# The query load of an attention kernel, cut into 120 partitions and 8 partitions

## The chip, the cores and the metric

One core of one Trainium2 chip runs the whole kernel. The metric is the device time of one execution in microseconds (us); lower is better. Times are medians of several runs. "Profile" is one profiled execution of a kernel; its span is a little shorter than the time (635.5 us for a time of 636.9). Some places below use the trace's raw records, which no view of the profile prints: the moment of each semaphore increment that a DMA makes, the start and duration of each DMA packet, and the queue of a packet. They are given in ordinary tables and in the text. The records do not name the DMA engine of a packet; where the text says that packets belong to one engine, that is inferred from their times, each packet starting where the one before it ends.

## The reference

```python
B, H, Sq, Skv, Dh = 8, 16, 16, 2048, 256          # all bfloat16, values of about 0.05
def reference(q, k, v):
    scale = q.shape[-1] ** -0.5
    scores = jnp.einsum('bhqd,bhkd->bhqk', q, k) * scale
    attn = _softmax(scores, axis=-1)
    return jnp.einsum('bhqk,bhkd->bhqd', attn, v)
```

There are 128 heads. Keys and values are 128 MiB each and are read once; the queries are 1 MiB, 8 KB for each head. So the kernel is a stream of key and value loads with the arithmetic hidden behind it.

## The kernel before

The 128 heads are taken in 16 groups of 8 ("g" below). Each group has two key loads and two value loads of 4096 KB (`u` counts them), the first four key loads being cut in halves and the last four value loads into smaller parts. Loads are issued on the queue of SP, in order, as soon as the buffer they fill is free. The query is loaded first, one head to a partition (one of the 128 rows of a buffer), into a buffer that the values use later; VectorE then transposes it.

```python
KN = ec(nc.sbuf_tensor("KN", [128, 2, NT, D], BF16))           # keys as loaded
KB = ec(nc.sbuf_tensor("KB", [128, R_KB, HT // 2, D], BF16))   # keys transposed, 4 slots
VB = ec(nc.sbuf_tensor("VB", [128, 2, NT, D], BF16))           # values
...
qx = q.rearrange("b h s d -> (b h) (s d)")                     # 128 rows of 8 KB
QR = VB[:, 1, 0:SQ, :].rearrange("p s d -> p (s d)")           # where they land
...
j_q = [J("sp", "ldq", lambda eng: eng.dma_start(QR[0:NH, :], qx), [j_qz], dma=(sem_q, 16))]
...
def k_load(u):                                                 # g: group of heads, e: 0 or 1
    g, e = u // 2, u % 2
    if g < 2:
        for h in range(2):
            j_k[u, h] = J("sp", "ld", lambda eng, h=h, n=HT: eng.dma_start(
                KN[:, e, HT * h:HT * h + HT, :], ku[u, :, HT * h:HT * h + HT, :]), ...)
...
j_qt[0] = J("dve", "qt", emit_qt, j_q)                         # transpose of the query
...
def kt(g, e, c):                                               # transpose of a quarter of a key load
    ...
    j_kt[g, e, c] = J("dve", "kt%d%d" % (e, c), lambda eng: emit_kt(eng, e, c), [j_k[2 * g + e, h], before])
```

`J` notes a job of an engine with the jobs it must wait for. Here all 128 heads exist, so `j_qz` is None and NH is 128.

## Time and profile before

| | before |
|---|---|
| time, median (lowest to highest) | 636.86 us (636.82 to 637.09, 4 runs) |
| span of the profile | 635.5 us |
| mean DMA rate over the span | 426 GB/s |
| one group of heads (16 MiB) | 39.0 us, 430 GB/s |

From the page of the kernel before: the share of the DMA engines that is busy in 40 equal slices (in tenths), the GB/s in each slice, and the chain of waits by engine.

```profile
DMA  8999999999999999999999999999999999999997
GB/s 364 430 432 437 442 431 429 433 429 431 431 431 431 431 429 433 429 433 429 433 430 431 433 429 433 429 429 433 437 425 439 435 429 439 427 440 429 414 424 280
...
DMA 74%; DVE 18%; issue 5%; PE 3%; SPq 0%; DVEq 0%; ACT 0%; ACTq 0%
```

The DMA engines are busy from end to end at some 430 GB/s, and three quarters of the chain of waits is DMA. The compute engines are not what the time waits for.

The start of the same kernel in stretches of 3 us (columns: length, busy time of each engine, TensorE clock, DMA share, GB/s). A packet's bytes are counted where the packet falls, so a single stretch can read a little over the true rate.

```profile
core 0: us, PE busy (x) PEld busy (x) DVE busy (x) ACT busy (x) POOL busy (x), PEclk, DMA share, GB/s
3.00:6.00 3.00, 0.00 (x0) 0.00 (x0) 0.00 (x0) 0.00 (x0) 1.91 (x1) 1.00 1.08 451
6.00:9.00 3.00, 0.00 (x0) 0.00 (x0) 1.90 (x1) 0.00 (x0) 0.00 (x0) 1.00 1.01 434
9.00:12.00 3.00, 0.00 (x0) 0.00 (x0) 2.82 (x6) 0.08 (x1) 0.00 (x0) 1.00 1.02 437
```

Already from 3 us on all DMA engines are busy (share 1.01 to 1.08) and the rate is full (434 to 451 GB/s). The end of the chain of waits (start, length, what):

```profile
591.84 30.00 DMA KN<-in_v_dram
621.84 0.14 issue
621.97 10.82 PE O_ps L183 x96
```

The last wait is for a part of a value load, which lands at 621.84 us; 96 matmuls follow without a gap. So the kernel ends some 14 us after that landing, and whatever moves the landing moves the end.

In these records each of the two loads raises its semaphore 16 times, and from 3 to 20 us 16 packets at a time are under way but for moments: one increment for each of 16 engines. These are the moments (us) for the first two loads, from the trace's records:

```
query load      5.25 ... 5.60 (15 increments)    7.01 (the last)
first key load  10.13 ... 10.49 (15 increments)  11.90 (the last)
```

One engine is 1.4 us behind the others from the query load on. By its times it is the one that also fetched 16 KB of instructions at 3.62 us: that packet of another queue took 961 ns, and the query packet behind it 773 ns instead of 309, together 1.43 us.

### The profile page before, as it was taken

The numbers are of one execution on the slowest core, as the hardware profiler recorded it, in microseconds if no ns is written. First come the engines' busy times: TensorE is split into PE (matmuls) and PEld (weight loads), VectorE is DVE, ScalarE is ACT, GpSimd is POOL, SyncE is SP. The second block draws the span as 40 slices with busy tenths as digits, with TensorE's granted clock in tenths as the row PEclk, the third lists the DMA queues.
The fourth block names the chain that finished last, engine by engine and source line by source line (L and its number), as shares of the span: only waits on it lengthen the run. The fifth ranks groups of instructions, "written<-read, shape, count | busy, mean of one in ns | idle before, by whom it ended". The sixth has DMA issues, their size and how long they took to land.

```text
span 635.5 us, 5055 instructions
## 1 busy us (share of the span) xinstructions
PE 485.9 (76%) x2176; PEld 165.5 (26%) x1680; DVE 437.5 (69%) x387; ACT 93.7 (15%) x176; POOL 4.2 (1%) x7
## 2 busy tenths in 40 slices
PE   0847859959598695976959679595895949959897
PEld 0101312214132141321313123131230412314286
DVE  6998894766938579395683947749477594766960
ACT  2030303003030030300303012030110302003010
POOL 2000000000000000000000000000000000000000
PEclk9969989969899698997979989699896998979999
DMA  8999999999999999999999999999999999999997
GB/s 364 430 432 437 442 431 429 433 429 431 431 431 431 431 429 433 429 433 429 433 430 431 433 429 433 429 429 433 437 425 439 435 429 439 427 440 429 414 424 280
DMA packets 13718, 270.62 MB, mean 426 GB/s; under 512 B 1552, under 2 KB 3856, under 8 KB 4368
## 3 DMA queue, kind: packets, MB, share of 16 engines
q1 hardware_dynamic: 13296, 270.36, 99.2%
q10 hardware_dynamic: 416, 0.18, 0.1%
q8 instruction: 4, 0.07, 0.0%
q14 instruction: 2, 0.02, 0.0%
HBM read 269.48 MB, written 1.05 MB: 426 GB/s over the span
## 4 chain that ended last, share of the span: by engine, by line
DMA 74%; DVE 18%; issue 5%; PE 3%; SPq 0%; DVEq 0%; ACT 0%; ACTq 0%
DMA KN<-in_k_dram 65%; DVE KB L133 16%; DMA KN<-in_v_dram 5%; DMA VB<-in_v_dram 4%; PE O_ps L183 2%; DVE QT L117 1%; PE S_ps L150 1%; PE S_ps L138 1%; DVE PC L163 0%; DVE negm L155 0%; SPq L217 0%; DVE O_fin L331 0%; SPq L201 0%; SPq L235 0%; DVEq L499 0%
## 5 line engine op out<-in xcount | busy, mean ns | idle before, releaser
L150 PE MATMUL S_ps<-KB,QW 128*128 128x512 bf16 x528 | 214.5, 415 | 136.5 <-DMA VB<-in_v_dram 94.3
L133 DVE STREAM_TRANSPOSE KB<-KN 128x2048 f32<-128x2048 f32 x128 | 284.8, 2280 | 48.6 <-DMA KN<-in_k_dram 47.8
L138 PE MATMUL S_ps<-KB,QW 128*128 128x512 bf16 x496 | 205.4, 414 | 0.0
L177 PE MATMUL O_ps<-VB,PT 128*128 128x512 bf16 x896 | 195.6, 379 | 9.3 <-DMA VB<-in_v_dram 9.3
L150 PEld LDWEIGHTS S_ps<-KB,QW 128*128 128x128 bf16 x528 | 54.0, 103 | 341.2 <-issue 278.6
L177 PEld LDWEIGHTS O_ps<-VB,PT 128*128 128x128 bf16 x896 | 86.7, 98 | 120.8 <-issue 18.1
L155 DVE TENSOR_REDUCE negm<-S_ps 128x1 f32<-128x2048 f32 x16 | 36.7, 2291 | 85.7 <-PE S_ps L138 85.7
L159 ACT ACTIVATE P_sb<-S_ps,negm 128x2048 bf16<-128x2048 f32 x16 | 31.5, 1967 | 409.3 <-DVE negm L155 409.3
L163 DVE STREAM_TRANSPOSE PC<-P_sb 128x1024 bf16<-128x1024 bf16 x32 | 37.9, 1222 | 33.8 <-ACT P_sb L159 33.8
L169 DVE COPY PT<-PC 32x1024 bf16<-32x1024 bf16 x128 | 53.4, 418 | 3.4 <-PE O_ps L183 1.7
L127 ACT ACTIVATE QW<-QT 32x128 bf16 (+1 forms) x128 | 53.9, 421 | 11.2 <-DVE QT L117 9.9
L320 ACT ACTIVATE O_tmp<-O_ps,rab 128x256 f32<-128x256 f32 x15 | 7.1, 473 | 96.3 <-PE O_ps L177 95.2
L183 PE MATMUL O_ps<-KN,PT 128*128 128x256 bf16 x128 | 14.5, 273 | 0.8 <-DMA KN<-in_v_dram 0.8
L183 PE MATMUL O_ps<-VB,PT 128*128 128x256 bf16 x128 | 14.1, 273 | 0.3 <-DVE PT L169 0.3
L183 PEld LDWEIGHTS O_ps<-KN,PT 128*128 128x128 bf16 x128 | 12.4, 98 | 2.7 <-issue 1.1
L183 PEld LDWEIGHTS O_ps<-VB,PT 128*128 128x128 bf16 x128 | 12.4, 98 | 2.3 <-DVE PT L169 0.8
L117 DVE COPY QT<-QN 32x512 f32<-32x512 f32 x16 | 9.7, 606 | 0.3
L331 DVE TENSOR_SCALAR O_fin<-O_ps,rab 128x256 bf16<-128x256 f32 x2 | 1.0, 482 | 12.5 <-PE O_ps L183 12.5
L325 DVE SCALAR_TENSOR_TENSOR O_fin<-O_ps,rab,O_tmp 128x256 bf16<-128x256 f32 x15 | 6.7, 445 | 1.8 <-issue 1.8
L110 DVE STREAM_TRANSPOSE QN<-VB 128x2048 f32<-128x2048 f32 x1 | 2.3, 2311 | 5.0 <-DMA VB<-in_q_dram 5.0
L302 DVE TENSOR_SCALAR rab<-mask,rinv 128x2 f32<-128x2 f32 x16 | 3.6, 228 | 2.1 <-DVE rinv L301 0.5
L196 POOL MEMSET PT<- 128x4096 f32 x1 | 3.5, 3511 | 0.0
(12 smaller groups left out, 10.8 us busy)
## 6 DMA issues: line engine op xcount, KB each, us to landing
VB<-in_v_dram SPq DMA_DIRECT2D x28, 4096.0 KB, 24.3
KN<-in_k_dram SPq DMA_DIRECT2D x28, 4096.0 KB, 30.0
KN<-in_k_dram SPq DMA_DIRECT2D x8, 2048.0 KB, 14.9
VB<-in_v_dram SPq DMA_DIRECT2D x4, 2048.0 KB, 17.1
KN<-in_v_dram SPq DMA_DIRECT2D x2, 2048.0 KB, 27.7
KN<-in_v_dram SPq DMA_DIRECT2D x2, 1024.0 KB, 24.3
KN<-in_v_dram SPq DMA_DIRECT2D x3, 512.0 KB, 26.9
VB<-in_q_dram SPq DMA_DIRECT2D x1, 1024.0 KB, 6.3
```

The source lines that it names most:

```text
L117: ins = eng.tensor_copy(dst[:, :, 8 * x:8 * x + 8], src[:, :, :, a])
L127: ins = eng.activation(ap_of(dv, dv.offset + 32 * a + e, [[256, 4], [128, 2], [2, 16]]), src.rearrange("p (s b) t -> p b t s", b=4), ACTF. ...
L133: return eng.transpose(KBf[:, c % R_KB].rearrange("p t i -> p (t i)"), KNf[:, e].rearrange("p t i -> p (t i)")[:, n * c:n * c + n])
L138: return eng.add_instruction(mybir.InstMatmult(start_tensor_calc=start, stop_tensor_calc=stop, ldweights=False, tile_size=(128, 128), tile ...
L150: ins = mm(S_ps[:, 2 * h + c, :], QW[:, e, bp, :], rhs, start=(e == 0 and bp == 0), stop=(e == 1 and bp == 7))
L155: return eng.tensor_reduce(out=negm[:], in_=S_ps[:].rearrange("p c n -> p (c n)"), axis=AX.X, op=ALU.max, negate=True)
L159: return eng.activation(P_sb[:], S_ps[:].rearrange("p c n -> p (c n)"), ACTF.Exp, bias=negm[:], scale=1.0, accum_out=lsum[:])
L163: return eng.transpose(PC[:, h].rearrange("p t x -> p (t x)"), P_sb[:, 1024 * h:1024 * h + 1024])
L169: ins = eng.tensor_copy(PT[pr, 32 * h:32 * h + 32, pr], PC[pr, h])
L177: ins = eng.matmul(O_ps[:, 0, :], PT[:, t, :], rhs, start=(t == 0), stop=(t == NT - 1))
L183: ins = eng.matmul(O_ps[:, bank, 0:D], PT[:, t, :], buf[:, t, :], start=(t == 0), stop=(t == NT - 1))
L320: j_ea[g] = J("act", "ea", lambda eng: eng.activation(O_tmp[:], src, ACTF.Copy, scale=rab[:, 0, 0:1]), [("pv", g, 1) if g < last - 1 else ...
```

## The change

The change text gives the intent as: the first 120 partitions' rows go over 15 DMA engines and the last 8 partitions' rows over 8. The natural purpose is to take the query rows away from one engine of the sixteen. Below it is called the spared engine, and the engines that carry the last 8 rows the eight.

```diff
-        j_q = [J("sp", "ldq", lambda eng: eng.dma_start(QR[0:NH, :], qx), [j_qz], dma=(sem_q, 16))]
+
+        j_q = [J("sp", "ldq", lambda eng, a=a, b=b: eng.dma_start(QR[a:b, :], qx[a:b]), [j_qz],
+                 dma=(sem_q, 32 if NH >= 120 else 16)) for a, b in ([(0, 120), (120, NH)] if NH >= 128 else [(0, NH)])]
```

## The prediction

> **What bounds the kernel now.** DMA throughput. The page's DMA row reads 9 tenths in nearly every slice at some 430 GB/s; the chain of waits is 74% DMA. One group of heads takes 39.0 us (spacing of the V-load issues on SP) for four 4096 KB loads: 430 GB/s. The queue never runs dry: a key load issued at 84.9 us lands 29.3 us later, three loads deep. At the end PE waits for the value load landing at 621.84 us, then runs 96 matmuls in 10.82 us without a gap.
>
> **The lag.** Each load lands as 16 semaphore increments, one per DMA engine. For the query load 15 come at 5.25 to 5.59 us and the last at 7.01 us. That engine lost its time to a 16 KB instruction fetch at 3.62 us (961 ns, and a query packet beside it took 773 ns instead of 309), and it stays 1.4 us behind: the next loads land with the same last gap. Later fetches hit other engines: one of 8 KB at 74.3 us puts a second 0.6 us back, and three of 16 KB at 590.8, 613.0 and 628.0 us put others about 1.3 us back. For the load landing at 621.84 us the last three engines stand at 621.67, 621.76 and 621.84.
>
> **What the change does.** [...] No engine numbers show in this trace; 120 partitions then give 15 engines and 8 give 8. So engine 15 gets no query row: it is spared 8 packets of 309 ns = 2.5 us, less some 0.5 us that it starts later, with the first key load, whose issue moves back by one DMA issue (0.4 us on SP). Engines 0 to 7 get one 8 KB row more, 0.31 us. Total bytes, PE, DVE and ACT work are unchanged.
>
> **What is on the critical path.** The slowest engine at the last loads. If the lagging engine is number 15 (the intent), it is no longer last: up to 1.4 us gained in most of the run, where the deep queue means nothing waits for it. At the end the engines hit by the fetches at 590 and 613 us are within 0.2 us of it, so only about 0.1 us is left to gain; if they are among engines 0 to 7 they come 0.31 us later than now. If the lagging engine is another, nothing is gained. A risk: 15-way splitting may make engines write the same part of the on-chip memory at once; doubling the query load's 2.5 us would put most engines, and the end, back by up to 2.5 us.
>
> **Prediction.** 637.0 us, range 636.3 to 638.6. Faster by over 2%: 0.5%; within 2%: 99%; slower: 0.5%.
>
> **What would show it.** Right: two query DMAs on SP, the first key load issued 0.4 us later; the last gap of 1.41 us of the first loads gone; the 39.0 us period, 430 GB/s and the PE tail of 10.8 us unchanged; the last loads moved by under 0.5 us. Wrong: query packets longer than 309 ns; a large last gap still there; the load before the PE tail landing over 0.5 us earlier or later; fetches at other times.
>
> **What would make it wrong.** A slow query load as said; the late fetches falling on the spared engine, which would let the whole 1.4 us through to the end; instruction fetches that move in time with the program.

The sum came to 637.0 us. Its terms are the 636.86 us before, less the 0.1 us left to gain at the end, plus 0.31 us for one packet of 8 KB (309 ns) more, together 637.07. "Engine 15" and "engines 0 to 7", here and in the expectations below, are names for the spared engine and for the eight; no trace shows an engine's number. The counts of 15 and 8 show in the trace after the change, in the next section. That engines which write the same part of the memory at once hold each other up was a guess here; what 8 rows to neighbouring partitions cost was measured later (+1.25 us, late8).

## The result, and the profile after

| | before | after |
|---|---|---|
| time, median (lowest to highest) | 636.86 us (636.82 to 637.09) | 640.18 us (640.12 to 640.34) |
| landing that the last 96 matmuls wait for | 621.84 us | 625.07 us |
| query packets of 8 KB, median | 309 ns | 610 ns |
| one group of heads | 39.0 us | 39.0 us |

The ratio of after to before is 1.0052 (95% interval 1.0034 to 1.0069). A ratio here is the mean time of one kernel's runs over that of the other's of the same rounds, so it is not quite the ratio of the medians quoted. The change makes the kernel 3.3 us slower, which is far outside the spread of the runs, though well under 2%.

The page of the kernel after:

```profile
DMA  8999999999999999999999999999999999999996
GB/s 285 430 434 428 435 434 437 431 431 429 431 427 431 433 433 431 439 431 433 427 433 427 431 429 431 438 437 431 435 431 429 427 431 429 431 438 435 416 425 277
...
DMA 70%; DVE 19%; issue 5%; PE 5%; SPq 0%; DVEq 0%; ACT 0%; ACTq 0%
```

Only the first slice differs much: 285 GB/s in place of 364. A slice is 16 us long. The busy row is the same digit for digit but for the last slice. The stretches show where in that slice:

```profile
core 0: us, PE busy (x) PEld busy (x) DVE busy (x) ACT busy (x) POOL busy (x), PEclk, DMA share, GB/s
3.00:6.00 3.00, 0.00 (x0) 0.00 (x0) 0.00 (x0) 0.00 (x0) 1.91 (x1) 1.00 1.03 243
6.00:9.00 3.00, 0.00 (x0) 0.00 (x0) 0.00 (x0) 0.00 (x0) 0.00 (x0) 1.00 1.00 218
9.00:12.00 3.00, 0.00 (x0) 0.00 (x0) 1.82 (x1) 0.00 (x0) 0.00 (x0) 1.00 1.01 421
```

From 3 to 9 us the DMA share is 1.0 as before, so the engines count as "busy", but they move 243 and 218 GB/s in place of 451 and 434. Over the 9 us from 3 to 12 us the sum of the three rates is 882 in place of 1322, so (1322 - 882) x 3 us = 1320 KB were not moved. At 430 GB/s these take 3.1 us. That is the whole loss: the end of the chain of waits is the same as before, moved by 3.2 us,

```profile
594.62 30.44 DMA KN<-in_v_dram
625.07 0.14 issue
625.20 10.77 PE O_ps L183 x96
```

and the middle has kept its period. On the SP queue two issues of value loads, eleven groups apart, before,

```profile
157.63 0.81 SPq L235 DMA_DIRECT2D VB<-in_v_dram  x2
...
586.88 1.82 SPq L235 DMA_DIRECT2D VB<-in_v_dram  x4
```

and after:

```profile
160.43 0.81 SPq L237 DMA_DIRECT2D VB<-in_v_dram  x2
...
589.67 1.81 SPq L237 DMA_DIRECT2D VB<-in_v_dram  x4
```

586.88 - 157.63 is 429.25 us and 589.67 - 160.43 is 429.24 us. Nothing was lost or won in between: this kernel streams at its DMA rate of some 430 GB/s throughout and made good none of the 3 us lost at its start.

VectorE sees the loss first. Its transpose of the query, with the idle time before it in brackets, before and after:

```profile
7.10 2.31 DVE L110 STREAM_TRANSPOSE QN<-VB 128x2048 f32<-128x2048 f32 x1 [5.03 <-DMA VB<-in_q_dram]
```

```profile
10.18 2.31 DVE L110 STREAM_TRANSPOSE QN<-VB 128x2048 f32<-128x2048 f32 x1 [8.11 <-DMA VB<-in_q_dram]
```

The increments after the change:

```
both query DMAs   1.31, 1.71 (2 increments, before any packet)   7.13 ... 10.09 (23 increments)
first key load    12.72   13.07 ... 13.76 (14 increments)   14.71 (the last)
```

From 3 to 5.1 us 15 packets at a time are under way after the change but for moments, where 16 were before; the sixteenth engine starts at 5.17 us, with the first key packet. So of the 23 late increments 15 are the first DMA's, and 8 are left for the second, one for each row. None of the 23 comes before 7.13 us, so the engine that began with keys at 5.17 us had no query row of either DMA: there is one spared engine, and the eight are among the other fifteen. The two early increments come before the first query packet starts (1.76 us). VectorE waits until the semaphore has risen by 32, 16 for each DMA, and is released at 10.18 us, after the last of the 23; so the two early ones stand for the missing 9. An engine that is late by about 1 us (14.71 against 13.76) is still there.

### The profile page after: what moved, and what is told of

It is laid out like the page before. It is cut to its first block, busy times and chain, and to the rows that moved or that the text cites. A ratio compares the mean times of both kernels' runs of the same rounds, so it can differ in the third digit from the quotient of the medians.

```text
span 638.6 us, 5056 instructions
## 1 busy us (share of the span) xinstructions
PE 488.1 (76%) x2176; PEld 165.8 (26%) x1680; DVE 437.6 (69%) x387; ACT 93.8 (15%) x176; POOL 4.2 (1%) x7
## 4 chain that ended last, share of the span: by engine, by line
DMA 70%; DVE 19%; issue 5%; PE 5%; SPq 0%; DVEq 0%; ACT 0%; ACTq 0%
DMA KN<-in_k_dram 61%; DVE KB L133 17%; DMA KN<-in_v_dram 5%; DMA VB<-in_v_dram 4%; PE O_ps L183 2%; PE S_ps L150 2%; PE S_ps L138 1%; DMA VB<-in_q_dram 1%; DVE QT L117 1%; DVE PC L163 0%; DVE QN L110 0%; DVE negm L155 0%; DVE O_fin L333 0%; SPq L202 0%; SPq L237 0%
```

## The experiments

**Theory P (place).** What a query packet takes depends on which partitions are written at the same time. With all 128 partitions in one DMA it is 309 ns (before); with 120 or 64 neighbouring ones twice that, as the 610 ns after the change suggest, with 8 neighbouring ones up to four times, and with 8 partitions that lie 4 apart nearly no delay. This was a conjecture. The author's grounds for it, how the rows of a DMA are dealt out to the engines and which partitions get in each other's way, are shown by no trace.

**Rivals.** I: the load is merely uneven (one engine with none, eight with one row more). D: a second DMA costs by itself, by its issue. K: a DMA that uses fewer than 16 engines is slow wherever it writes. One more was not named before the runs, H: what counts is the place in memory that the rows are read from, not the partitions that they are written to. S came with the last pair: what extra8_spread lost besides was due not to the place but to an engine that stood idle.

The runs below were made in three batches, each on a chip of its own and each against the kernel before on that chip. Its median was 636.96 us (9 runs) in the first batch (halves, only120, extra8, extra_tiny), 637.08 in the second (columns, extra8_spread, spread8, block8) and 637.02 in the third (late8, late8_spread); the row "after" is the change itself, against 636.86.

| run | what it is | time, median | over before |
|---|---|---|---|
| after | 120 rows, then 8 rows | 640.18 | +3.3 |
| halves | 64 rows, then 64 rows | 639.74 | +2.8 |
| columns | 128 rows twice, half a row each | 637.79 | +0.7 |
| only120 | 120 rows, the rest not loaded | 639.17 | +2.2 |
| extra8 | as before, 8 rows more to 8 neighbouring partitions | 638.20 | +1.2 |
| extra8_spread | the same 8 rows to 8 partitions 4 apart | 638.08 | +1.0 |
| extra_tiny | as before, 128 pieces of 512 bytes more | 637.39 | +0.4 |
| spread8 | 16 DMAs of 8 rows, partitions 4 apart | 645.29 | +8.2 |
| block8 | 16 DMAs of 8 rows, neighbouring partitions | 650.91 | +13.8 |
| late8 | extra8, issued after the first key loads | 638.27 | +1.25 |
| late8_spread | extra8_spread, issued there | 637.34 | +0.3 |

For columns, extra8_spread, extra_tiny and late8_spread the 95% interval of the ratio includes 1, so by that measure these four can't be told from before; of them only the runs of extra8_spread overlap with those of before.

### Two halves of 64 partitions: no engine is spared

```diff
-        j_q = [J("sp", "ldq", lambda eng: eng.dma_start(QR[0:NH, :], qx), [j_qz], dma=(sem_q, 16))]
+        j_q = [J("sp", "ldq", lambda eng, a=a: eng.dma_start(QR[a:a + 64, :], qx[a:a + 64]), [j_qz], dma=(sem_q, 32))
+               for a in (0, 64)]
```

> The query load as rows 0 to 63 and rows 64 to 127, each of 64 partitions[...]: no engine is spared, none has more than before. Theory P [...]: query packets of about 612 ns instead of 309, the first key load lands about 2.5 us later, the whole kernel +2.5 us (639.4). Rival I (imbalance: the loss came from the extra row on engines 0 to 7 and from a spared engine that started late): packets 309 ns, total within 0.3 us of before. Rival D (each further DMA on the queue costs by itself): about +0.4 us.

Measured: 639.74 us, ratio 1.0043 (1.0029 to 1.0056), query packets of 600 ns in the median. The first two stretches of the start:

```profile
3.00:6.00 3.00, 0.00 (x0) 0.00 (x0) 0.00 (x0) 0.00 (x0) 1.91 (x1) 1.00 1.03 235
6.00:9.00 3.00, 0.00 (x0) 0.00 (x0) 0.00 (x0) 0.00 (x0) 0.00 (x0) 1.00 1.03 273
```

At a DMA share of 1.03 in both stretches no engine can have stood idle for long, and the rate is far down all the same: 235 and 273 GB/s in place of 451 and 434. Rival I, which asked for packets of 309 ns, can't give this. Rival D asked for +0.4. How the 64 rows are dealt out to the engines is not shown.

### Two halves by columns: two DMAs of all 128 partitions

```diff
-        j_q = [J("sp", "ldq", lambda eng: eng.dma_start(QR[0:NH, :], qx), [j_qz], dma=(sem_q, 16))]
+        j_q = [J("sp", "ldq", lambda eng, a=a: eng.dma_start(QR[:, a:a + 2048], qx[:, a:a + 2048]), [j_qz], dma=(sem_q, 32))
+               for a in (0, 2048)]
```

> The query load in two DMAs as in the change, but cut along the columns: both have all 128 partitions, 4 KB of each. Same bytes, same number of DMAs as the change and as the halves. Theory P: [...] packets are 159 ns for 4 KB as elsewhere, and the end is within 0.4 us of before. Rival D (a second query DMA costs by itself, by its issue or by being one more to finish): +2.5 us as with the halves.

Measured: 637.79 us (637.69 to 637.92), ratio 1.0011 (0.9997 to 1.0025), packets of 4 KB at 159 ns in the median.

```profile
3.00:6.00 3.00, 0.00 (x0) 0.00 (x0) 0.00 (x0) 0.00 (x0) 1.91 (x1) 1.00 1.07 365
6.00:9.00 3.00, 0.00 (x0) 0.00 (x0) 1.46 (x1) 0.00 (x0) 0.00 (x0) 1.00 0.97 401
9.00:12.00 3.00, 0.00 (x0) 0.00 (x0) 2.92 (x5) 0.00 (x0) 0.00 (x0) 1.00 1.02 437
```

The same bytes in the same number of DMAs cost 0.7 us instead of 2.8. That is against rival D as the main cause. It is more than the 0.4 us that was expected, though: some 0.8 us worth of bytes is missing between 3 and 9 us ((1322 - 365 - 401 - 437) x 3 us = 357 KB). Why is not settled; about a third of these packets was longer than 159 ns.

### Each part of the change alone

The first part alone (the last quadrant of the transposed query is made from another quadrant's rows):

```diff
+        j_q = [J("sp", "ldq", lambda eng: eng.dma_start(QR[0:120, :], qx[0:120]), [j_qz], dma=(sem_q, 16))]
...
-            return eng.transpose(QN[:].bitcast(F32), QR.bitcast(F32))
+            eng.transpose(QN[0:96, :].bitcast(F32), QR[0:96, :].bitcast(F32))
+            return eng.transpose(QN[96:128, :].bitcast(F32), QR[64:96, :].bitcast(F32))
```

> Rows 0 to 119 alone on 15 engines; the last 8 rows are not loaded and the last quadrant is filled from another one (a wrong result on purpose, one more transpose of 2.3 us on the vector engine at the start, where it has slack). The first part of the change alone. Theory P: packets of about 612 ns, first key load about +2.5 us on 15 engines, the end about +2.4 us: most of the 3.3 us of the change. Rival I: packets 309 ns, nothing later than before, the end within 0.2 us. If the spared engine were the one that lags, its increment would come first, not last, at the first key load; if not, the last gap of about 1 us stays.

Measured: 639.17 us (639.08 to 640.12), ratio 1.0035 (1.0021 to 1.0049), query packets 572 ns. The result even passed the comparison, presumably because the scores are so small that other queries hardly change the softmax. The query load's last increment came at 9.61 us, 1.76 us after the one before it, on the engine that fetched 16 KB at 4.20 us. That engine had query rows, so the lagging engine is not the spared one. Two reservations: the profiled run was the slowest of the five (640.12 us), with a second engine late at the first key load (13.46 us, where most stand at 12.30 to 12.60); and no engine was done with its query rows before 7.25 us (5.25 before the change). So whatever slows the packets reached all 15 engines; the next run shows something of the same kind.

The second part alone, into spare memory (slot 3 of KB, which is written only after VectorE has waited for `sem_q`):

```diff
+        QD = KB[120:128, 3].rearrange("p t i -> p (t i)")
+        j_q = [J("sp", "ldq", lambda eng: eng.dma_start(QR[0:NH, :], qx), [j_qz], dma=(sem_q, 32)),
+               J("sp", "ldq", lambda eng: eng.dma_start(QD, qx[120:128]), dma=(sem_q, 32))]
```

> The query load whole as before, then the last 8 rows once more into spare memory, as an 8-partition DMA on 8 engines. This is the second part of the change alone. Theory P: [...] engines 0 to 7 come out some 1.2 to 1.5 us later at the first key load, the others little; the end +0.1 us if the engines that fetch late are not among them, up to +1.5 us if they are. Rival I: they come out 0.3 us later, the end at most +0.3 us.

Measured: 638.20 us (638.14 to 638.26), ratio 1.0019 (1.0005 to 1.0033).

The two parts add up: 2.2 + 1.2 = 3.4 us, against 3.3 us for the change. But extra8 did not go as theory P had it in detail. The eight were to be late and the others hardly. In fact 15 increments of the first key load came at 11.29 to 11.82 us, against 10.13 to 10.49 before: all engines lost about 1.1 us, because the first key packets behind the query rows took 1.2 to 1.6 us instead of 0.61, on engines with and without one of the 8 rows (all but the lagging one, which got there later). So 8 rows to 8 neighbouring partitions held up nearly all engines. The path by which it happens is not shown here.

### A control: one more small DMA of all 128 partitions

```diff
+        QD = KB[:, 3, 0, :]
+        j_q = [J("sp", "ldq", lambda eng: eng.dma_start(QR[0:NH, :], qx), [j_qz], dma=(sem_q, 32)),
+               J("sp", "ldq", lambda eng: eng.dma_start(QD, qx[:, 0:D]), dma=(sem_q, 32))]
```

> The query load whole as before, then a further DMA of 128 partitions with 512 bytes each into spare memory: a control for what one more DMA costs by being issued. Theory P: query packets stay 309 ns, the end within 0.4 us of before (64 KB more are 0.15 us and 8 small packets for each engine 0.2 us). Rival D: +2 us or more, since the first key load waits behind one more issue.

Measured: 637.39 us (637.30 to 637.49), ratio 1.0007 (0.9993 to 1.002), query packets 309 ns. The +0.4 us is at the edge of what was expected. Rival D falls.

### The 8 rows to partitions 4 apart, twice

The edit against extra8:

```diff
-        QD = KB[120:128, 3].rearrange("p t i -> p (t i)")
+        QD = KB[96:125:4, 3].rearrange("p t i -> p (t i)")
```

> As extra8, but the 8 extra rows go to partitions 96, 100 and so on to 124, [...] instead of 120 to 127[...]. Same 8 engines, same bytes, same issue. Theory P: the first key load's increments move by some 0.3 to 0.5 us instead of the 1.1 us of extra8, and the end is some 0.3 to 0.6 us over before instead of 1.24. Rival K (a DMA on fewer than 16 engines, or one that starts while others run, costs that much wherever it writes): the same 1.1 and 1.24 us again.

Measured: 638.08 us, but spread from 637.38 to 638.41; ratio 1.0013 (0.9999 to 1.0027). At the first key load theory P held: 14 increments at 10.59 to 10.87 us, 0.4 us over before and not 1.1. The end did not follow, because in the profiled run (638.41 us) a second engine was 1.2 us late there. By the times of its packets it stood idle from 5.05 to 6.09 us, until its first key packet came. The issue was not quite the same either: the extra DMA took 0.83 us on SP instead of 0.36, so the first key load was issued at 2.06 us instead of 1.59 in extra8. As a whole time this run is inconclusive. So the pair was run again with the 8 rows behind the first two key loads, where no engine was expected to run dry (late8 against before; late8_spread has the other QD, partitions 96, 100 and so on to 124):

```diff
+        QD = KB[120:128, 3].rearrange("p t i -> p (t i)")
         for g in range(G):
             for u in (2 * g, 2 * g + 1):
                 k_load(u)
+                if u == 0:
+                    j_x = J("sp", "ldq", lambda eng: eng.dma_start(QD, qx[120:128]), dma=(ec(nc.semaphore("s_x")), 16))
...
-            j_kt[g, e, c] = J(..., [j_k[2 * g + e, h], before])
+            j_kt[g, e, c] = J(..., [j_k[2 * g + e, h], before, j_x if (g, e, c) == (0, 0, 3) else None])
```

> The query load whole as before; the 8 extra rows of extra8 (partitions 120 to 127[...]) are issued only after the first two key loads, so that no engine can run dry at the start. Theory P: the increments of the first key load stay where they are before the change (10.1 to 10.5 us and the late one), those of the third load come some 1.0 us later on most engines than before the change, and the end is +1.0 to 1.2 us. Rival K: the same as late8_spread.

> As late8[...]. Theory P: the third load's increments come only some 0.15 to 0.35 us later than before the change, the end +0.15 to +0.4 us. Rival S [...] is the same theory in full: here no engine runs dry, so the bimodal 637.4 to 638.4 us of extra8_spread should be gone.

Measured: late8 638.27 us (638.12 to 638.29), ratio 1.0019 (1.0006 to 1.0033); late8_spread 637.34 us (637.27 to 637.54), ratio 1.0006 (0.9992 to 1.0019). The stretch from 15 to 18 us, in which the 8 rows and the load behind them fall, of before, late8 and late8_spread:

```profile
15.00:18.00 3.00, 1.45 (x4) 0.39 (x3) 2.60 (x2) 0.39 (x1) 0.00 (x0) 1.00 1.02 437
```

```profile
15.00:18.00 3.00, 1.60 (x4) 0.39 (x3) 1.53 (x2) 0.22 (x1) 0.00 (x0) 1.00 0.90 284
```

```profile
15.00:18.00 3.00, 1.44 (x4) 0.39 (x3) 2.20 (x2) 0.38 (x1) 0.00 (x0) 1.00 1.00 399
```

The two kernels read the same 8 rows, with the same shape and the same place in the queue (the issue took 0.72 and 0.83 us); only the 8 destination partitions differ. So rival H falls for these rows: what they cost depends on where they are written. The neighbouring partitions cost 153 GB/s over 3 us (437 - 284), the ones 4 apart 38. The third key load's 15 early increments stand at 19.93 to 20.28 us before, 21.04 to 21.69 in late8 and 20.45 to 20.93 in late8_spread. Rival K falls: the same 8 rows cost +1.25 us in neighbouring partitions and +0.3 us in partitions 4 apart. The third load moved by 0.5 to 0.65 us in late8_spread, twice what was expected at most, but the end only by 0.3 us, as expected; late8's end is just over its 1.0 to 1.2 us. The spread of the times is gone (637.27 to 637.54), as rival S expected; that the engine which ran dry made the spread was seen in one profile only.

For the 120 rows there is no such pair: in every run that writes other partitions at once, other rows are read at once too. That the partitions written and not the source cost the +2.2 us is carried over from this pair and from the doubled packets, and is not shown by a run of its own.

### The whole query by 8 engines, neighbouring partitions or not

```diff
# spread8: 8 partitions, 4 apart
+        j_q = [J("sp", "ldq", lambda eng, a=a: eng.dma_start(QR[a:a + 29:4, :], qx[a:a + 29:4]), [j_qz], dma=(sem_q, 256))
+               for a in (0, 1, 2, 3, 32, 33, 34, 35, 64, 65, 66, 67, 96, 97, 98, 99)]
# block8: 8 neighbours
+        j_q = [J("sp", "ldq", lambda eng, a=a: eng.dma_start(QR[a:a + 8, :], qx[a:a + 8]), [j_qz], dma=(sem_q, 256))
+               for a in range(0, 128, 8)]
```

> The query load as 16 DMAs of 8 partitions, 4 apart, each on 8 engines[...]. Engines 0 to 7 carry all the query rows, 16 each, and 16 issues take some 7 us on the queue. Theory P: packets near 309 ns; the query load done some 7 to 9 us after its start (bound by the issue), the end some 3 to 6 us over before. Rival K: as block8.

> The same 16 DMAs on the same 8 engines, but of 8 neighbouring partitions each[...]: only which partitions meet in a DMA differs from spread8. Theory P: packets of some 600 to 1240 ns [...], the query load takes up to 20 us, and the end is some 8 to 17 us over before, well over spread8. Rival K: packets and time as spread8.

Measured: spread8 645.29 us (ratio 1.0131), packets 419 ns in the median; block8 650.91 us (ratio 1.0218), packets 943 ns in the median. Block8 fell where theory P put it. Its first stretch:

```profile
3.00:6.00 3.00, 0.00 (x0) 0.00 (x0) 0.00 (x0) 0.00 (x0) 1.91 (x1) 1.00 0.48 66
```

A DMA share of 0.48 is 8 of 16 engines, all busy, and they move 66 GB/s together. From 7.3 us the first key load runs on the eight engines without query rows, and until the query load ends at 19.78 us most of its 16 KB packets took 1.1 to 2.5 us there instead of 0.61. That is extra8's finding again, on a larger scale. Spread8 is a miss in size, 8.2 us where 3 to 6 were expected. Its 16 issues took 10.9 us on SP (0.7 us each, not the 0.4 us reckoned), so the first key load was issued at 11.64 us instead of 1.18; in block8 the issues took 5.5 us. Its packets were longer than 309 ns too; why was not looked into. So the two differ in more than the partitions, and the sizes can't be compared closely; but block8, with the shorter issue, has packets of over twice the length and the longer time, as theory P says.

Spread8 tells one thing more. Its query rows all go by the same eight engines, if it is as in block8, where 16 DMAs of 8 rows kept a DMA share of 0.48; and its instruction fetch runs from 2.18 to 3.23 us. All eight packets of the first query DMA ran in that time (from 2.29 to 2.97 us), and its eight increments stand at 3.15 to 3.29 us: the fetch has delayed none of them. (The first key load's 16 increments stand within 0.35 us of each other, but these engines had idle time before it in which to catch up.) So the engine that fetches there is none of the eight. With only120 (it is not the spared one) that leaves the seven others, if DMAs of 8 rows use the same eight engines in every run, and if the same engine fetches in every run; no run here shows an engine's number. Which of them it is was not tried.

## Why the prediction was wrong

The prediction said 637.0 us with a range of 636.3 to 638.6; it was 640.18.

- **The step that failed: the price of the query load.** The prediction put it at its bytes, "Engines 0 to 7 get one 8 KB row more, 0.31 us", and left the rest of the load at its old 309 ns a packet. The runs put it at 610 ns a packet. Engines that write the same part of the memory at once stood in the text only as a risk, "doubling the query load's 2.5 us would put most engines, and the end, back by up to 2.5 us", outside the sum, and that bound lay outside the range as well. It was the main term: only120 measures it as +2.2 us and halves as +2.8 us. That the packets doubled is measured; that the partitions written at once are the reason is shown for the last 8 rows and argued from there for the 120.
- **The second term, the last 8 rows,** was priced as one row more on each of the eight, 0.31 us. Extra8 and late8 measure +1.2 us: 8 rows in 8 neighbouring partitions, which held up engines that had none of them. In partitions 4 apart it is +0.3 us (late8_spread).
- **The lagging engine.** The condition "If the lagging engine is another, nothing is gained" is what happened: a large last gap stayed (0.95 us at the first key load after the change), and only120 excludes the spared engine and spread8 the eight, on the two conditions named there. The spared engine was of no use.
- **"At the end ... only about 0.1 us is left to gain"** was right in kind. Spread8 has no lagging engine at the first key load, yet at the load that the last 96 matmuls wait for, its last increment still comes 1.7 us after its first (1.9 us before the change). So removing the first lag would not have closed that gap; the later fetches (at 590.80 and 612.99 us before the change) are the likely reason.
- **What was right:** the DMA rate of some 430 GB/s that bounds the kernel, the unchanged 39.0 us period, the unchanged matmuls at the end, the issue of the first key load 0.4 us later, and that what the engines lose at the start comes back in full at the end: 1320 KB not moved are 3.1 us, and the landing moved by 3.2 us.

No run points to a version that beats the kernel before. The query load in one DMA of 128 partitions was the fastest of all that were tried.

## What to carry to other kernels

Before cutting a load by partitions, look at what its packets take; here the full 128 partitions ran at 309 ns a packet, and 120, 64 or 8 neighbouring ones at 572, 600 and 943 ns. If a load must be cut, cutting it along the columns was the cheaper way here (+0.7 us against +2.8). An instruction fetch of 16 KB put one engine back by 1.4 us here, and it stayed that far behind in the loads that followed (16.80 us against 15.38, 21.69 against 20.28, before the change). And read GB/s beside the DMA share: a share of 1.0 went with 434 GB/s before the change and with 218 after it, so the busy row alone hides a halved rate.
